# Strided extra keys in slots of their own, and one more product of 288 columns for them

## The chip, the cores and the metric

One Trainium2 chip, one of its cores. The metric is device microseconds of one execution. The kernel before takes 358.15 us, the median of 3 runs (357.57 to 358.64).

## The reference, cut to what matters

Three layers stand one behind the other. The first is attention with two masks, the second a soft mixture of experts, the third a dense layer pair with an ELU between.

```python
mask_local = (rel >= 0) & (rel < 32)                                   # heads 0 to 3
mask_strided = (rel >= 0) & (pos[None, :] % 32 == pos[:, None] % 32)   # heads 4 to 7
...                                    # softmax, attn @ v: 4 batches, 8 heads, 576 x 64
logits = x @ phi                       # 2304 x 512 by 512 x 32
slot_input = softmax(logits, 0).T @ x  # 32 slots, 4 for each of 8 experts
h = relu(slot_input[e] @ w1[e]); slot_out[e] = h @ w2[e]     # 512 -> 1024 -> 512
x = softmax(logits, 1) @ slot_out
h = x @ w_in                           # 2304 x 512 by 512 x 2048
g = where(h > 0, h, exp(min(h, 0)) - 1)
out = g @ w_out
```

In a strided head a query sees only keys of its own residue modulo 32. There are 576 / 32 = 18 keys for each residue, so a strided unit works on residues: 18 queries by 18 keys for each residue and batch.

## The kernel before, in words

All of it is one straight program. The attention is cut into 20 units, 12 local (L) and 8 strided (S), in the order `LLSLLLSSSLSSLSSLLLLL`. A unit goes through these steps: scores on TensorE (`f_qk`, L542, for a local one, two halves `f_qks`, L561, for a strided one), a softmax on VectorE and ScalarE, the division and for a strided unit the packing into `pst` on GpSimd (`f_mul`, L628), a 32x32 block transpose on VectorE (`f_tr`, L636 and L639), four copies into a block-diagonal tile `bd` on ScalarE and GpSimd (`f_sp`, L657 and L659), the products with V on TensorE (`f_pv`, L670, local; `f_pvs`, L683, strided) and the copy out of PSUM. There are two `bd` tiles for all units, three PSUM tiles `t` for the strided products and the transposes of the result, and two tiles each for scores and local products.

A strided unit holds 16 residues. Each one's 18 keys lie in 32 slots: keys 0 to 15 in the even slots, keys 16 and 17 in slots 1 and 17. V of the residue lies in the same rows of its tile, so the tile has two extra rows per batch among odd rows that are zero. These extra rows come by a load of their own (L239): 32 partitions of 2048 columns, of which three in four are zeros. One group of the product (`f_pvs(g)`) is four residues by two halves of the unit, each a product of 128 rows by 72 columns; the two halves write partitions 0 to 63 and 64 to 127 of one PSUM tile.

When the result of all units of a third of the tokens is there, TensorE makes the logits (L777) and transposes it in place (L786). Then follow the slot inputs (L413, L910), the experts' first layer (L923), their second layer (`emit_w2`, L1012) for experts 0 to 7 one behind the other, and the dense layers from L1153 on, which take the rest of the time.

The order of the work in the attention is set by a planner (`list_order`): each node has an engine, a cost, the nodes that it waits for and a key, and on each engine the ready node with the lowest key among those that can start next comes first. The keys come from a unit's due time `T[n] = T0 + TP * n + TD[n]`. The planner sets the order of the instructions alone; on the chip each engine runs its own list in that order and waits where data is missing.

All loads are issued by the sync engine, in one list. A weight load goes into a slot that an earlier tile held, and waits for the last reader of that tile: experts 1 and 2, for instance, wait for the strided scores and for the products of the first strided head pair (`q_of`, `v_of`). The dense layer's first columns (`load_head`, L348) go into the last 512 columns of four of these slots. The last weight load before the dense layers is that of expert 7's second matrix, in five parts.

Of the kernel before, what the change touches and what calls it, by code (L numbers as in the profile page):

```python
# [13 lines left out]
ALU = mybir.AluOpType  # L14
# [5 lines left out]
def attn_moe_mlp(ctx, tc, q, k, v_l, v_s, phi, w1, w2, w_in, w_out, out):  # L20
    nc = tc.nc
# [8 lines left out]
    RES = 32  # L30
    MR = S // RES
# [10 lines left out]
    T0, TP, AE = 6.0, 2.89, 0.1  # L42
    TD = (
        -32.4, -12.6, -3.1, -2.4, -7.2, 0.6, -6.0, -3.7, 1.6, -4.1,
        -0.9, -5.9, 1.6, 4.2, -2.1, 2.3, 7.2, -3.3, -9.5, 0.3,
# [31 lines left out]
    QW, WB = S * B, 4096  # L77
# [156 lines left out]
    def load_v(p, a, b):  # L234
        if p < 2:
            nc.sync.dma_start(out=VT[p][:, a:b], in_=v_l[p, :, a:b])
        else:
            nc.sync.dma_start(out=VT[p][0:128:2, a:b], in_=v_s[p - 2, 0:64, a:b])
            nc.sync.dma_start(out=VT[p][1:128:4, a:b], in_=v_s[p - 2, 64:96, a:b])  # L239
# [16 lines left out]
    with tc.manual_schedule():  # L256
# [180 lines left out]
        for n, (p, t, h) in enumerate(units):  # L437
            if p < 2:
                u = 2 * t + h
                lo_hi[n] = {"q": (384 * u, 384 * u + 384), "k": (max(384 * u - 128, 0), 384 * u + 384)}  # L440
                lo_hi[n]["v"] = lo_hi[n]["k"]
            else:
                c = 1152 * t + 576 * h
                lo_hi[n] = {"q": (c, c + 576), "k": (c, c + 576), "v": (2048 * t + 1024 * h, 2048 * t + 1024 * h + 1024)}

# [7 lines left out]
        lt = [an("G", d, [], x, f) for d, x, f in zip((0.95, 1.15, 1.15, 0.55, 1.5, 1.8), (12.0, 11.0, 11.1, 13.0, 30.0, 9.5), late)]  # L453
        RATE = 2.42
        post = []

        def load_node(kind, p, a, b, after=(), pre=None):
            f = {"q": load_q, "k": load_k, "v": load_v}[kind]
            if pre is not None:
                f = lambda *a: None  # L460
            need = min(users(p, kind, a, b))
            key = T[need] - (14 if kind != "v" else 9)
            dur = 128 * 4 * (b - a) / 1e6 * RATE
            if kind == "v" and p >= 2:
                dur *= 0.63
                after = [("n", y) for (k_, x), y in lv.items() if k_ == p and a <= x < b]
            post.append((key if pre is None else pre, dur, after, lambda: f(p, a, b), (kind, p, a, b)))
# [9 lines left out]
        for p in (2, 3):  # L477
            for x in range(2):
                h = (HW_ * x, HW_ * x + HW_)
                load_node("q", p, *h, pre=-70.0 if p == 2 and x == 0 else None)  # L480
                if p == 2 and x == 0:
                    load_node("v", p, 0, 2048)
                    continue
                load_node("k", p, *h, after=[("qk", n) for n in users(2, "k", *h)] if p == 3 else [("n", y) for y in lt[1:3]])
                load_node("v", p, 2048 * x, 2048 * x + 2048)
        for x in range(2):
            h = (HW_ * x, HW_ * x + HW_)
            load_node("q", 1, *h, after=[("qk", n) for n in users(2, "q", *h)])
            load_node("k", 1, *h, after=[("qk", n) for n in users(0, "k", *h)])
            load_node("v", 1, *h)  # L490
# [30 lines left out]
        head_node(2.5, 1, [])  # L521
# [5 lines left out]
        def unit_nodes(n):  # L527
# [91 lines left out]
            def f_mul():  # L619
# [7 lines left out]
                for a, b, o in ((0, 16, slice(0, 32, 2)), (16, MR, slice(1, 32, 16))):  # L627
                    nc.gpsimd.tensor_tensor(  # L628
                        out=z["pin"][:, :, o], in0=z["s"][:, :, a:b], in1=sm.to_broadcast([128, 16, b - a]), op=ALU.mult
                    )  # L630
# [44 lines left out]
            def f_pvs(g):  # L675
                def f():
                    pt = z["bd"]
                    og = z["o", g] = ps_t.tile([128, 512], F32, tag="t", name="so")[:, 0:4 * B * MR]
                    for j in range(4):
                        c0 = B * MR * j  # L680
                        r = 4 * g + j
                        for hh in range(2):
                            nc.tensor.matmul(  # L683
                                og[64 * hh:64 * hh + 64, c0:c0 + B * MR], v_t[p][:, t, h, hh, r, :],
                                pt[:, 8 * hh + r].rearrange("p (b m) -> p b m", b=B)[:, :, 0:MR], start=True, stop=True,
                            )
# [60 lines left out]
            vd = [x for x, y in data if y[1] == p and y[0] == "v" and n in users(p, "v", y[2], y[3])]  # L747
# [9 lines left out]
            for g in range(2):  # L757
                r = []
                y = an("P", 0.62, sp + vd, K - 7.3 + 0.6 * g, f_pvs(g), ("t", r), 32)
# [618 lines left out]
_INS = ['q', 'k', 'v_l', 'v_s', 'moe_phi', 'moe_w1', 'moe_w2', 'moe2_w_in', 'moe2_w_out']  # L1378
# [3 lines left out]
def _lay(np, q, k, v, moe_phi, **rest):  # L1382
# [10 lines left out]
    vs = v[:, 4:8].reshape(B, 2, 2, S // 32, 2, 2, 8, D).transpose(1, 0, 3, 4, 5, 2, 6, 7).reshape(2, B, S // 32, 64 * D)  # L1393
    x, z = vs[:, :, 16:], np.zeros_like(vs[:, :, 16:])
    vs = np.concatenate([x.reshape(2, -1, 64 * D) for x in (vs[:, :, 0:16], np.stack([x, z, z, z], axis=3))], axis=1)
# [4 lines left out]
    return dict(rest, q=lay(q), k=lay(k), v_l=vl, v_s=vs, moe_phi=phi, moe_w1=w1, moe_w2=w2)  # L1400
# [25 lines left out]
```

## Time and profile before

| | |
|---|---|
| median of 3 runs | 358.15 us |
| the profiled execution's own time | 357.83 us |
| its span, from the first to the last instruction | 356.1 us |
| TensorE busy | 336.8 us (95%), 2678 matmuls |
| VectorE, ScalarE, GpSimd busy | 260.8, 248.7, 57.4 us |
| moved by DMA | 70.50 MB |
| granted TensorE clock, mean | 0.998 of full speed |

Times in the rows are microseconds from the start of the span. A TensorE float32 matmul of the program shows as two matmuls in the trace (two passes), so "x32" at L683 is 16 products. A matmul's duration holds its run through the array, so several overlap; the start of the next group says how long one really holds the engine. "X idle before <-Y" is how long the engine stood still ahead of the piece, and what ended it. For a DMA, "us to landing" runs from its issue to the arrival of its last byte, with all that lies ahead of it in the queue.

### The profile page before, as it was taken

The numbers are of one execution on the slowest core, as the hardware profiler recorded it, in microseconds if no ns is written. First come the engines' busy times: TensorE is split into PE (matmuls) and PEld (weight loads), VectorE is DVE, ScalarE is ACT, GpSimd is POOL, SyncE is SP. The second block draws the span as 40 slices with busy tenths as digits, with TensorE's granted clock in tenths as the row PEclk, the third lists the DMA queues.
The fourth block names the chain that finished last, engine by engine and source line by source line (L and its number), as shares of the span: only waits on it lengthen the run. The fifth ranks groups of instructions, "written<-read, shape, count | busy, mean of one in ns | idle before, by whom it ended". The sixth has DMA issues, their size and how long they took to land.

```text
span 356.1 us, 6955 instructions
## 1 busy us (share of the span) xinstructions
PE 336.8 (95%) x2678; PEld 249.6 (70%) x2678; DVE 260.8 (73%) x574; ACT 248.7 (70%) x488; POOL 57.4 (16%) x106
## 2 busy tenths in 40 slices
PE   5589899998999999999999999999999999999995
PEld 4378777773333257787888788888878888888884
DVE  6999889743706069999999999997755674576741
ACT  9588999982216079999977877767656666666650
POOL 8888534520214000000000000000000000000000
PEclk9999999999999999999999999999999999999999
DMA  7999999999999998750006041000000030032301
GB/s 280 401 418 411 424 421 421 424 407 420 430 424 417 404 403 323 250 221 0 3 0 238 0 162 74 2 0 0 2 0 1 2 119 0 31 118 88 118 2 59
DMA packets 15328, 70.50 MB, mean 198 GB/s; under 512 B 1600, under 2 KB 2112, under 8 KB 12352
## 3 DMA queue, kind: packets, MB, share of 16 engines
q1 hardware_dynamic: 15296, 70.06, 49.3%
q8 instruction: 21, 0.34, 0.4%
q14 instruction: 11, 0.09, 0.1%
HBM read 65.34 MB, written 4.72 MB: 197 GB/s over the span
## 4 chain that ended last, share of the span: by engine, by line
PE 74%; DVE 8%; DMA 6%; ACT 4%; POOL 4%; issue 2%; DVEq 0%; SPq 0%; POOLq 0%
PE ops L1312 18%; PE ops L1314 18%; PE ops L1313 18%; DMA q<-in_moe_w_dram 6%; PE hps L1264 5%; PE s_ps L923 3%; ACT bd L657 2%; DVE sc L589 2%; PE o_ps L670 2%; PE mps L1153 1%; ACT xw L696 1%; PE xtps L786 1%; DVE sm L613 1%; POOL bd L659 1%; DVE ss L604 1%
## 5 line engine op out<-in xcount | busy, mean ns | idle before, releaser
L1274 DVE SCALAR_TENSOR_TENSOR g<-hps,g 128x512 f32<-128x512 f32 (+1 forms) x80 | 50.7, 634 | 17.8 <-ACT g L1271 17.3
L1268 ACT ACTIVATE g<-hps 128x512 f32<-128x512 f32 (+1 forms) x80 | 44.8, 560 | 13.6 <-PE hps L1264 12.2
L1271 ACT ACTIVATE g<-g 128x512 f32<-128x512 f32 (+1 forms) x80 | 47.5, 594 | 1.5
L1280 ACT ACTIVATE ghi<-g 128x512 fp32r<-128x512 f32 (+1 forms) x40 | 23.7, 591 | 18.3 <-DVE g L1274 16.5
L1314 PE MATMUL ops<-w,glo 128*128 128x512 f32 (+1 forms) x93 | 36.0, 387 | 0.0
L1280 ACT ACTIVATE rings<-g 128x512 fp32r<-128x512 f32 (+1 forms) x39 | 23.6, 606 | 17.3 <-DVE g L1274 16.5
L1312 PE MATMUL ops<-wh,rings 128*128 128x512 f32 x80 | 31.6, 396 | 0.0
L1312 PE MATMUL ops<-w,ghi 128*128 128x512 f32 (+1 forms) x81 | 31.4, 388 | 0.0
L1313 PE MATMUL ops<-w,ghi 128*128 128x512 f32 (+1 forms) x81 | 31.4, 387 | 0.0
L1313 PE MATMUL ops<-wl,rings 128*128 128x512 f32 x80 | 31.2, 390 | 0.0
L1314 PE MATMUL ops<-wh,glo 128*128 128x512 f32 x80 | 31.2, 390 | 0.0
L1264 PE MATMUL hps<-pers 128*128 128x512 f32 (+1 forms) x80 | 30.3, 380 | 0.0
L657 ACT ACTIVATE bd<-tr 32x288 f32<-32x288 f32 (+1 forms) x60 | 28.7, 479 | 1.3
L1313 PE MATMUL ops<-w,rings 128*128 128x512 f32 x64 | 25.0, 391 | 0.0
L1312 PE MATMUL ops<-w,rings 128*128 128x512 f32 x64 | 25.0, 391 | 0.0
L1314 PE MATMUL ops<-wh,rings 128*128 128x512 f32 x62 | 24.3, 392 | 0.0
L1312 PE MATMUL ops<-wh,ghi 128*128 128x512 f32 x62 | 24.2, 391 | 0.0
L1313 PE MATMUL ops<-wl,ghi 128*128 128x512 f32 x62 | 24.2, 391 | 0.0
L1314 PE MATMUL ops<-w,rings 128*128 128x512 f32 x52 | 20.2, 389 | 0.0
L1284 DVE TENSOR_TENSOR glo<-g,ghi 128x512 fp32r<-128x512 f32 (+1 forms) x24 | 15.2, 633 | 6.8 <-ACT ghi L1280 4.5
L1314 PEld LDWEIGHTS ops<-w,glo 128*128 128x128 f32 x93 | 17.5, 188 | 3.6
L670 PE MATMUL o_ps<-bd,v 128*64 128x128 f32 x288 | 18.1, 276 | 1.2 <-ACT bd L657 0.9
(230 smaller groups left out, 757.8 us busy)
## 6 DMA issues: line engine op xcount, KB each, us to landing
v<-in_moe_w_dram SPq DMA_DIRECT2D x3, 2048.0 KB, 11.8
w<-in_moe_w_in_dram SPq DMA_DIRECT2D x3, 2048.0 KB, 8.0
out_dram<-ob SPq DMA_DIRECT2D x17, 256.0 KB, 2.0
w<-in_moe_w_dram SPq DMA_DIRECT2D x2, 2048.0 KB, 11.6
xw<-in_moe_w_dram SPq DMA_DIRECT2D x4, 1024.0 KB, 11.9
xw<-in_moe_w_out_dram SPq DMA_DIRECT2D x2, 2048.0 KB, 7.8
q<-in_q_dram SPq DMA_DIRECT2D x6, 576.0 KB, 8.0
kB<-in_k_dram SPq DMA_DIRECT2D x8, 288.0 KB, 7.5
```

The source lines that it names most:

```text
L657: nc.scalar.activation(out=o, in_=i, func=AF.Copy)
L670: nc.tensor.matmul(o[64 * e:64 * e + 64, j, :], v_t[p][:, max(i - 1 + k, 0), e, :], pt[:, 4 * j + 2 * e + k], start=(k == 0), stop=(k == 1),)
L923: nc.tensor.matmul(hp[32 * g:32 * g + 32, :], siT[:, POS[c], :], w_at(2 * a + g // 2, 0, 2 * c + g % 2), start=(c == CO[0]), stop=(c == CO ...
L1264: nc.tensor.matmul(t["ps"], M4[:, 128 * f:128 * f + 128], cTf[:, t0:t0 + n], start=True, stop=True)
L1268: nc.scalar.activation(out=t["g"], in_=t["ps"], func=AF.Exp)
L1271: nc.scalar.activation(out=t["g"], in_=t["g"], func=AF.Relu, scale=-1.0, bias=1.0)
L1274: nc.vector.scalar_tensor_tensor(out=t["g"], in0=t["ps"], scalar=0.0, in1=t["g"], op0=ALU.max, op1=ALU.subtract)
L1280: nc.scalar.activation(out=t["hi"], in_=t["g"], func=AF.Copy)
L1284: nc.vector.tensor_tensor(out=t["lo"], in0=t["g"], in1=t["hi"].bitcast(F32), op=ALU.subtract)
L1312: nc.tensor.matmul(o[:, x], t["hi"][:, c], hi[:, x], start=(f == f0), stop=False)
L1313: nc.tensor.matmul(o[:, x], t["hi"][:, c], lo[:, x], start=False, stop=False)
L1314: nc.tensor.matmul(o[:, x], t["lo"][:, c], hi[:, x], start=False, stop=(f == f1 - 1 and x.stop == 512))
```

## The change

The extra keys 16 and 17 of a residue get slots that differ by residue: residue r of a group of eight takes the odd slots 2r+1 and 2r+17. So no two of eight residues share an odd slot, and the extra V rows of eight residues fit together in one compact tile of 64 columns for each half (`VX`, four tiles of 256 columns, the odd partitions; even ones are zero). A group of the strided product then begins with one more product for each half, 128 rows by 288 columns (the four residues' columns at once), and the eight products of 72 columns add to it. The odd rows of V's own tile are zero now. The 32-partition load of 2048 columns (four times) goes; a 64-partition load of 256 columns (four times) comes. Two GpSimd memsets clear the compact tiles. The fourth compact tile lies in columns 4096 to 4351 of the slot of `v2`, which was the place of the first dense columns; their load waits for the last strided product now, and its place in the list is later. The planner has a new cost for the strided product and other due times.

```diff
-    T0, TP, AE = 6.0, 2.89, 0.1
+    T0, TP, AE = -0.1, 2.858, 0.1
...
-            nc.sync.dma_start(out=VT[p][0:128:2, a:b], in_=v_s[p - 2, 0:64, a:b])
-            nc.sync.dma_start(out=VT[p][1:128:4, a:b], in_=v_s[p - 2, 64:96, a:b])
+            nc.sync.dma_start(out=VT[p][0:128:2, a:b], in_=v_s[p - 2, :, a:b])
+
+    vx = small("xt", 768, "vx", 1)
+    VX = {(2, 0): vx[:, 0:256], (2, 1): vx[:, 256:512], (3, 0): vx[:, 512:768], (3, 1): v2_sb[:, WB:WB + 256]}
+
+    def load_x(p, a, b):
+        nc.sync.dma_start(out=VX[p, a // 256][1:128:2, :], in_=v_x[p - 2, :, a:b])
...
+        lx = [an("G", 0.72, [], 9.0, lambda: nc.gpsimd.memset(vx, 0.0))]
+        lx += [an("G", 0.3, lx, 14.2, lambda: nc.gpsimd.memset(VX[3, 1], 0.0))]
...
-        head_node(2.5, 1, [])
+        head_node(5.7, 1, v_of(3))
...
-                for a, b, o in ((0, 16, slice(0, 32, 2)), (16, MR, slice(1, 32, 16))):
-                    nc.gpsimd.tensor_tensor(
-                        out=z["pin"][:, :, o], in0=z["s"][:, :, a:b], in1=sm.to_broadcast([128, 16, b - a]), op=ALU.mult
-                    )
+                nc.gpsimd.tensor_tensor(
+                    out=z["pin"][:, :, 0:32:2], in0=z["s"][:, :, 0:16], in1=sm.to_broadcast([128, 16, 16]), op=ALU.mult
+                )
+                d = z["pin"]
+                d = bass.AP(tensor=d.tensor, offset=d.offset + 1, ap=[d.ap[0], [256, 2], [34, 8], [16, MR - 16]])
+                nc.gpsimd.tensor_tensor(
+                    out=d, in0=z["s"][:, :, 16:MR].rearrange("p (e r) x -> p e r x", e=2),
+                    in1=sm.rearrange("p (e r) x -> p e r x", e=2).to_broadcast([128, 2, 8, MR - 16]), op=ALU.mult,
+                )
...
+                    cx = VX[p, t][:, 128 * h:128 * h + 128]
+                    for hh in range(2):
+                        nc.tensor.matmul(
+                            og[64 * hh:64 * hh + 64], cx[:, 64 * hh:64 * hh + 64],
+                            pt[:, 8 * hh + 4 * g:8 * hh + 4 * g + 4].rearrange("p r (b m) -> p r b m", b=B)[:, :, :, 0:MR],
+                            start=True, stop=False,
+                        )
...
-                                pt[:, 8 * hh + r].rearrange("p (b m) -> p b m", b=B)[:, :, 0:MR], start=True, stop=True,
+                                pt[:, 8 * hh + r].rearrange("p (b m) -> p b m", b=B)[:, :, 0:MR], start=False, stop=(j == 3),
...
-                y = an("P", 0.62, sp + vd, K - 7.3 + 0.6 * g, f_pvs(g), ("t", r), 32)
+                y = an("P", PVS, sp + vd, K - 7.3 + 0.6 * g, f_pvs(g), ("t", r), 40)
```

The planner's new due times change the order on all engines in the attention. Behind the product L910 TensorE's order is the same in both programs. On TensorE, from the second local value product to the first two groups of the strided one, the kernel before has these rows (`s_ps` scores, `o_ps` and `so` local and strided products with V, `lg` logits, `xtps` transposes of the result):

```order
L670 MATMUL o_ps_99<-bd,v_83 64x128 x12
L561 MATMUL s_ps_97<-kB,ex 64x72 x8
L561 MATMUL s_ps_96<-kB,ex 64x72 x8
L777 MATMUL lg<-xw,phi 32x192 x4
L786 MATMUL xtps<-ident,xw 128x128 x6
L683 MATMUL so<-bd,v_105 64x72 x8
L542 MATMUL s_ps_97<-kA,q_103 32x128 x12
L683 MATMUL so<-bd,v_105 64x72 x8
```

and the changed one these:

```order
L689 MATMUL o_ps_99<-bd,v_83 64x128 x12
L556 MATMUL s_ps_97<-kA,q_103 32x128 x12
L803 MATMUL lg<-xw,phi 32x192 x4
L812 MATMUL xtps<-ident,xw 128x128 x6
L689 MATMUL o_ps_98<-bd,v_83 64x128 x12
L575 MATMUL s_ps_96<-kB,ex 64x72 x8
L700 MATMUL so<-bd,vx 64x288 x2
L709 MATMUL so<-bd,v_105 64x72 x8
L700 MATMUL so<-bd,vx 64x288 x2
L709 MATMUL so<-bd,v_105 64x72 x8
```

The two rows L700 are new, and 16 such rows stand in the program. Ahead of the first strided product there are now three local value products (L689) and six local score blocks (L556) instead of two and five (L670, L542), and five strided score halves (L575) instead of six (L561).

On the sync engine, the weight loads of the attention's second half stand like this before (`w` expert 0, `ex` the two halves of expert 1, `v_105` expert 2 in the slot of `v2`, `kB` expert 3, `q_103` expert 4, `v_106` expert 5 in the slot of `v3`, `v_83` a part of expert 6; 512 columns of `w_in` are the dense layer's first columns):

```order
L363 DMA w_740<-in_moe_w_dram 128x4096
L363 DMA ex<-in_moe_w_dram 128x2048
L348 DMA v_105<-in_moe_w_in_dram 128x512
L348 DMA q_103<-in_moe_w_in_dram 128x512
L363 DMA v_83<-in_moe_w_dram 128x2048
L363 DMA v_105<-in_moe_w_dram 128x4096
L363 DMA ex<-in_moe_w_dram 128x2048
L363 DMA kB<-in_moe_w_dram 128x4096
L363 DMA q_103<-in_moe_w_dram 128x4096
L363 DMA v_106<-in_moe_w_dram 128x4096
```

and now like this:

```order
L369 DMA w_662<-in_moe_w_dram 128x4096
L231 DMA kB<-in_k_dram 64x1152 x2
L226 DMA q_104<-in_q_dram 128x1152
L369 DMA ex<-in_moe_w_dram 128x2048
L354 DMA q_103<-in_moe_w_in_dram 128x512
L369 DMA v_83<-in_moe_w_dram 128x2048
L369 DMA ex<-in_moe_w_dram 128x2048
L369 DMA kB<-in_moe_w_dram 128x4096
L369 DMA v_105<-in_moe_w_dram 128x4096
L369 DMA q_103<-in_moe_w_dram 128x4096
L369 DMA v_106<-in_moe_w_dram 128x4096
L354 DMA kB<-in_moe_w_in_dram 128x512
```

Expert 2's load of 2 MB (`v_105`) has moved behind the second half of expert 1 (`ex`) and expert 3 (`kB`), which both wait for the last strided scores.

## Rows read from the trace of the kernel before

**Rows 1.** Chain that ended last: start, length, engine, tile, line.

```profile
89.77 7.07 PE s_ps L923 x64
...
101.08 0.29 SPq L363
101.41 22.16 DMA q<-in_moe_w_dram
123.62 2.34 PE o_ps L1012 x8
```

**Rows 2.** Windows: stretch, length, busy time by engine (instructions), clock, DMA share, GB/s.

```profile
5.00:25.00 20.00, 12.50 (x273) 10.66 (x273) 17.88 (x58) 14.66 (x28) 17.20 (x22) 1.00 1.02 406
25.00:65.00 40.00, 36.44 (x788) 30.01 (x786) 36.21 (x113) 37.48 (x83) 22.11 (x42) 1.00 1.02 420
65.00:80.00 15.00, 14.94 (x211) 11.40 (x208) 8.25 (x34) 13.75 (x33) 7.32 (x11) 1.00 0.99 411
...
126.00:356.00 230.00, 226.22 (x1054) 181.63 (x1053) 179.20 (x320) 166.82 (x319) 0.00 (x0) 1.00 0.22 83
```

**Rows 3.** Timeline of TensorE, experts' second layer: start, length, line, shapes.

```profile
113.30 1.90 PE L1012 MATMUL o_ps<-ex,h1T_b 128*32 128x512 f32 x16
115.01 1.90 PE L1012 MATMUL o_ps<-v,h1T_b 128*32 128x512 f32 x16
...
118.04 1.07 PE L1012 MATMUL o_ps<-kB,h1T_b 128*32 128x512 f32 x8
...
120.74 1.05 PE L313 MATMUL wps<-ident 128*128 128x256 bf16 x8
121.72 1.66 PE L1012 MATMUL o_ps<-q,ss 128*32 128x512 f32 x8
...
125.89 0.83 PE L313 MATMUL wps<-ident 128*128 128x256 bf16 x6
```

**Rows 4.** Page, section 6: DMA issues, count, KB each, median us to landing.

```profile
out_dram<-ob SPq DMA_DIRECT2D x17, 256.0 KB, 2.0
...
v<-in_v_s_dram SPq DMA_DIRECT2D x4, 256.0 KB, 7.8
...
phi<-in_moe_phi_dram SPq DMA_DIRECT2D x1, 64.0 KB, 5.6
```

**Rows 5.** Timeline of TensorE in the attention.

```profile
18.92 0.67 PE L561 MATMUL s_ps<-kB,ex 128*64 128x72 f32 x16
19.52 0.86 PE L542 MATMUL s_ps<-kA,q 128*32 128x128 f32 x24
20.31 1.53 PE L670 MATMUL o_ps<-bd,v 128*64 128x128 f32 x24
21.68 0.67 PE L561 MATMUL s_ps<-kB,ex 128*64 128x72 f32 x16
...
25.77 0.72 PE L683 MATMUL so<-bd,v 128*64 128x72 f32 x16
...
63.75 1.22 PE L683 MATMUL so<-bd,v 128*64 128x72 f32 x32
64.80 1.48 PE L670 MATMUL o_ps<-bd,v 128*64 128x128 f32 x24
```

**Rows 6.** Timeline of GpSimd, a memset of 768 columns.

```profile
0.80 0.74 POOL L260 MEMSET kA<- 128x768 f32 x1 [0.29 <-POOLq L1410]
```

**Rows 7.** Page, section 5: ScalarE's copies into the block-diagonal tile.

```profile
L657 ACT ACTIVATE bd<-tr 32x288 f32<-32x288 f32 (+1 forms) x60 | 28.7, 479 | 1.3
```

**Rows 8.** Timeline of the sync engine: issues of weight loads.

```profile
51.02 0.33 SPq L363 DMA_DIRECT2D ex<-in_moe_w_dram  x1
...
93.44 0.33 SPq L363 DMA_DIRECT2D w<-in_moe_w_dram  x1
```

**Rows 9.** DMA issues of the windows 50:60 and 93.4:93.6, those two loads' landing.

```profile
ex<-in_moe_w_dram SPq DMA_DIRECT2D x1, 1024.0 KB, 9.1
...
w<-in_moe_w_dram SPq DMA_DIRECT2D x1, 2048.0 KB, 11.4
```

More of the change, by code (lines that the diff above doesn't have):

```diff
@@ L19, in attn_moe_mlp @@
 @with_exitstack
-def attn_moe_mlp(ctx, tc, q, k, v_l, v_s, phi, w1, w2, w_in, w_out, out):
+def attn_moe_mlp(ctx, tc, q, k, v_l, v_s, v_x, phi, w1, w2, w_in, w_out, out):
     nc = tc.nc
@@ L30, in attn_moe_mlp @@
     RES = 32
+    PVS = 1.1
     MR = S // RES
@@ L41, in attn_moe_mlp @@
     FIFO = ("sp", "sl", "ss", "cb", "pst", "mx", "sm", "tr", "bd", "o", "qw", "t", "l")
-    T0, TP, AE = 6.0, 2.89, 0.1
+    T0, TP, AE = -0.1, 2.858, 0.1
     TD = (
-        -32.4, -12.6, -3.1, -2.4, -7.2, 0.6, -6.0, -3.7, 1.6, -4.1,
-        -0.9, -5.9, 1.6, 4.2, -2.1, 2.3, 7.2, -3.3, -9.5, 0.3,
+        -35.5, -18.2, -0.3, -9.8, -1.4, 0.8, -3.0, -3.4, 4.9, -9.2,
+        -6.5, 5.9, -3.5, 4.1, -1.0, 4.2, 4.4, -1.2, -4.4, 8.0,
     )
@@ L441, in attn_moe_mlp @@
                 lo_hi[n]["v"] = lo_hi[n]["k"]
+                lo_hi[n]["x"] = (0, 0)
             else:
@@ L444, in attn_moe_mlp @@
                 lo_hi[n] = {"q": (c, c + 576), "k": (c, c + 576), "v": (2048 * t + 1024 * h, 2048 * t + 1024 * h + 1024)}
+                lo_hi[n]["x"] = (256 * t + 128 * h, 256 * t + 128 * h + 128)
         def users(p, kind, a, b):
@@ L457, in load_node @@
         def load_node(kind, p, a, b, after=(), pre=None):
-            f = {"q": load_q, "k": load_k, "v": load_v}[kind]
+            f = {"q": load_q, "k": load_k, "v": load_v, "x": load_x}[kind]
             if pre is not None:
@@ L461, in load_node @@
             need = min(users(p, kind, a, b))
-            key = T[need] - (14 if kind != "v" else 9)
+            key = T[need] - {"v": 9.0, "x": 8.9}.get(kind, 14.0)
             dur = 128 * 4 * (b - a) / 1e6 * RATE
+            if kind == "x":
+                dur *= 0.53
             if kind == "v" and p >= 2:
-                dur *= 0.63
+                dur *= 0.5
                 after = [("n", y) for (k_, x), y in lv.items() if k_ == p and a <= x < b]
@@ L482, in attn_moe_mlp @@
                     load_node("v", p, 0, 2048)
+                    load_node("x", p, 0, 256, after=[("n", lx[0])])
                     continue
@@ L485, in attn_moe_mlp @@
                 load_node("v", p, 2048 * x, 2048 * x + 2048)
+                load_node("x", p, 256 * x, 256 * x + 256, after=[("n", lx[p == 3 and x == 1])])
         for x in range(2):
@@ L746, in unit_nodes @@
             rel["tr"] += sp
-            vd = [x for x, y in data if y[1] == p and y[0] == "v" and n in users(p, "v", y[2], y[3])]
+            vd = [x for x, y in data if y[1] == p and y[0] in "vx" and n in users(p, y[0], y[2], y[3])]
             if local:
@@ L1375, in attn_moe_mlp @@
             nodes[n][4]()
-_INS = ['q', 'k', 'v_l', 'v_s', 'moe_phi', 'moe_w1', 'moe_w2', 'moe2_w_in', 'moe2_w_out']
+_INS = ['q', 'k', 'v_l', 'v_s', 'v_x', 'moe_phi', 'moe_w1', 'moe_w2', 'moe2_w_in', 'moe2_w_out']
 _OUTS = [((2304, 512), 'float32')]
@@ L1391, in _lay @@
     vl = v[:, 0:4].reshape(B, 2, 2, S // 32, 32, D).transpose(1, 0, 4, 3, 2, 5).reshape(2, 128, 4 * S)
-    vs = v[:, 4:8].reshape(B, 2, 2, S // 32, 2, 2, 8, D).transpose(1, 0, 3, 4, 5, 2, 6, 7).reshape(2, B, S // 32, 64 * D)
-    x, z = vs[:, :, 16:], np.zeros_like(vs[:, :, 16:])
-    vs = np.concatenate([x.reshape(2, -1, 64 * D) for x in (vs[:, :, 0:16], np.stack([x, z, z, z], axis=3))], axis=1)
+    vs = v[:, 4:8].reshape(B, 2, 2, S // 32, 2, 2, 8, D).transpose(1, 0, 3, 4, 5, 2, 6, 7)
+    vx = vs[:, :, 16:].transpose(0, 1, 2, 6, 3, 4, 5, 7).reshape(2, 64, 8 * D)
+    vs = vs[:, :, 0:16].reshape(2, 64, 64 * D)
     phi = moe_phi.reshape(4, 128, -1).transpose(1, 0, 2).reshape(128, -1)
@@ L1399, in _lay @@
               for w in (rest["moe_w1"], rest["moe_w2"]))
-    return dict(rest, q=lay(q), k=lay(k), v_l=vl, v_s=vs, moe_phi=phi, moe_w1=w1, moe_w2=w2)
+    return dict(rest, q=lay(q), k=lay(k), v_l=vl, v_s=vs, v_x=vx, moe_phi=phi, moe_w1=w1, moe_w2=w2)
 def kernel(**inputs):
```

## The prediction, before the changed kernel ran

> **What bounds the kernel now.** I read the chain of waits first, from its end backwards. From 123.62 on it is TensorE almost without a break [rows 1], busy 226.22 of the 230 us behind 126 [rows 2]; the change touches nothing there, so what counts is when that part begins. Just ahead of it the chain leaves TensorE: the sync engine issues expert 7's second matrix at 101.08, as soon as its slot is free, and the data take 22.16 us [rows 1]. That is a queue, not a slow transfer: the windows show all DMA engines full from 5 on (share 0.99 to 1.02, 406 to 420 GB/s) [rows 2]. So the start of the dense part is set by bytes ahead of that matrix over rate.
>
> TensorE runs close behind. In the second layer an undisturbed expert takes 115.01 - 113.30 = 1.71 us. Expert 6 takes 120.74 - 118.04 = 2.70, and expert 7, from 121.72 to the next work at 125.89, 4.17 [rows 3]. The excess, 0.99 + 2.46 = 3.45 us, is all that TensorE waits for weights, since the fillers (L313) between are in the program anyway. So two paths lead to 125.89: the loads, with no slack, and TensorE from the attention on, with 3.45 us. The third view is the attention in windows: TensorE is busy 12.50 of 20 us in 5 to 25, 36.44 of 40 in 25 to 65 and 14.94 of 15 in 65 to 80. In the first stretch VectorE is nearly full (17.88 of 20), in the second ScalarE (37.48 of 40) [rows 2].
>
> **The change part by part.** *Loads.* Four loads of 256 KB [rows 4] become four of 64 KB (64 partitions, 256 columns, 4 bytes: an estimate from the shapes), 0.79 MB less, at 420 GB/s 1.87 us. Count and issue time on the sync engine stay, since one issue replaces one. A small load isn't free in itself, but in a full queue it costs its bytes: that of phi, 64 KB, landed in 5.6 us, no later than a 256 KB load (7.8) [rows 4]. The Trainium skill speaks against this part: DMA: Bandwidth & Descriptors, section Bandwidth, has 64 KB transfers at 0.95 us and calls smaller ones descriptor-dominated. By that figure, an estimate, four would take 3.8 us and the loads would lose 1.3 instead of gaining 1.9; the row of phi doesn't show it.
>
> *The new products.* 16 groups get one product of 288 columns for each of two halves. Bounds: the first layer's 512-column products take 7.07 us for 64 passes, four at a time, 0.44 a round [rows 1]; 288 columns in two passes are then 0.50 us with the halves side by side. The eight old products of a group hold the engine (64.80 - 63.75) / 2 = 0.525 for the same columns per half [rows 5]; if the halves ran one behind the other it would be about 1.0. I take 0.50, as the nearest row also streams wide: 16 x 0.50 = 8.0 us more on TensorE, all between 25 and 70. The upper end is 16.
>
> *What hides of that.* First, the new order. Ahead of the first strided product TensorE has now done one local score block more (20.31 - 19.52 = 0.79), one local value block more (21.68 - 20.31 = 1.37) and one strided score half less (19.52 - 18.92 = 0.60) [rows 5]: 1.56 us of work drawn into a stretch with idle time. This holds if that product comes no later than 25.77 [rows 5]; VectorE has 12 instructions more ahead of its transpose, at most 12 x 17.88 / 58 = 3.7 us [rows 2], but before, the product came some time behind it. GpSimd (17.20 of 20 busy) gets two memsets, 0.74 for 768 columns [rows 6] and a third of that for 256: 1.0 us. I put 0.4 us on the first product for both, between 0 and 3. Second, idle time behind 25: 40 - 36.44 + 15 - 14.94 = 3.6 us [rows 2]. It goes only where ScalarE has the next tile ready. The product holds its `bd` tile twice as long, and the copies into the next one (4 x 0.479 us [rows 7]) can't begin sooner. I let 1.0 of the 3.6 stay, between 0 and 3.6. So the attention ends 8.0 - 1.56 + 0.4 - 2.6 = 4.2 us later (bounds 2.8 and 9.4, by these edits alone).
>
> *Moved loads.* Expert 2's 2 MB now stand behind two loads that wait for the last strided scores. On the sync engine all later weights queue behind such a wait. The load issued at 51.02 [rows 8] landed 9.1 later, 1 MB [rows 9]: less 2.5 for its own bytes at 420 GB/s and about 1.4 of latency (256 KB on an empty queue land in 2.0 us [rows 4], 0.6 of it bytes), 5.2 us lay ahead of it. Expert 2 (5.0), a head of dense columns (0.6) and the saving (1.87) are missing there now, 7.5 us: if the scores come at the same time, the queue stands empty for 2.3 us, which eats the saving. They stand earlier in TensorE's list by work, so I take a hole of 0 to 2.3, 0.8 likely. The load at 93.44 landed 11.4 later, 2 MB, so 11.4 - 5.0 - 1.4 = 5.0 us lay ahead [rows 8, 9]; with TensorE 4.2 later and the queue 1.87 less a hole of 0.8 earlier the slack is gone and 0.3 us of hole come. So the loads end 1.87 - 0.8 - 0.3 = 0.8 us earlier. The dense columns' own load, moved behind, is read only after the first layer (from 89.77 [rows 1]) and bytes ahead of expert 7 stay the same: nothing. The division's other pattern on GpSimd writes as many elements: nothing, at most 0.2 a unit, under the same cover of ScalarE.
>
> *Sum.* The dense part begins when the later path ends: loads -0.8, TensorE 4.2 - 3.45 = +0.75. TensorE becomes the bound. On the profiled execution that is 357.83 + 0.75 = 358.6 (span 356.1 and 1.7 around it, as now); the median shown lies 0.3 above the profiled time, so I predict **358.9 us**. About 0.3%, 1.07 us, is what a measurement of this kernel can tell from no change.
>
> **Rivals.** *Slower: the second tile isn't ready.* Place: `bd` copies on ScalarE between 25 and 65. For it: two tiles for all units, ScalarE busy 94% there [rows 2]; against: ScalarE gets 4 us more time for the same work. If none of the idle time is used the attention ends 8.0 - 1.56 + 0.4 = 6.8 us later, the dense part 3.4: 361.5. It decides from 3.45 + 1.07 = 4.5 us late.
>
> *Faster: the products are hidden.* If more early work is drawn forward (7.5 us stand idle in 5 to 25 [rows 2]) and the rest of the idle time is used, TensorE ends less than 1.6 us late and the bytes decide: 358.15 - 1.87 = 356.3. For it: the order was moved as a whole; against: VectorE is full in that stretch and its work is the same, and TensorE alone has no idle time behind 65.
>
> *No gain by the queue.* TensorE is in time, but the hole at 51 takes the saving: 358.15 + 2.3 - 1.87 = 358.6. For it: the 7.5 against 5.2 us above; against: the scores need be only 2.3 us earlier.
>
> *Small loads hold the queue.* If the four new loads cost what the old ones did, nothing is saved: the loads end 1.87 later than in the sum, 1.1 behind now, and the time is 359.2 by rows, at the edge of the bound. Against: phi's row [rows 4]. By the page named above they would lose 1.3 us more, which gives 360.5.
>
> *The halves don't overlap.* The wide products cost 16 us instead of 8, and the time is 8 us above the forecast, 367. Against: the 72-column pairs do overlap on the same halves, as their 0.525 us a group shows [rows 5].
>
> **How the numbers follow.** Forecast 0.43 (358.0 to 359.9; 0.31 of it within the bound, 0.12 slower), tile not ready 0.23 (slower), hidden 0.20 (faster), the queue 0.10 (same), small loads 0.02 (slower), no overlap 0.02 (slower). That gives faster 0.20, same 0.41, slower 0.39. The range for 8 in 10 reaches from the hidden case to just short of the full slow one, 356.4 to 361.3; the forecast's own is 358.0 to 359.9.
>
> **What would show it.** The new products: 32 products (64 matmuls) at about 0.25 us a pass, 0.50 a group. The attention: the first matmul of the experts' first layer, now at 89.77, at about 94. The second layer: experts 6 and 7 at 1.71 us each, without waits for DMA. The loads: expert 7's matrix there before TensorE asks. Wrong would be an attention that ends less than 2 or more than 6 us later, DMA waits still at experts 6 and 7 (then the loads bound it), or a DMA share well under 1 between 48 and 56 (then the queue's hole).

## The result, and the profile after

The changed kernel takes 363.31 us (median of 4 runs, 362.50 to 363.63), the one before 358.15 beside it (median of 3; a fourth execution, of 383.28, is a slow one and left out): ratio 1.0142, 95% interval 1.0113 to 1.0170, slower by 4.1 to 6.1 us. Predicted were 358.9 us, 356.4 to 361.3. The profiled execution took 363.12 us, 5.29 more than that of before, and the dense part begins 5.27 later. Behind that start nothing changed: the profiled time less the start is 231.9 to 232.1 us in the kernels below, so each can be read by when its dense part begins.

The windows of after, columns as in [rows 2]:

```profile
5.00:25.00 20.00, 15.59 (x278) 12.94 (x280) 17.26 (x57) 14.10 (x26) 17.12 (x23) 1.00 1.01 393
25.00:65.00 40.00, 35.84 (x752) 29.28 (x751) 35.09 (x112) 34.36 (x76) 21.33 (x42) 1.00 0.96 390
65.00:80.00 15.00, 14.65 (x220) 10.78 (x222) 5.49 (x17) 13.76 (x29) 8.30 (x13) 1.00 0.93 371
...
126.00:356.00 230.00, 229.77 (x1078) 181.77 (x1071) 177.72 (x317) 166.84 (x319) 0.00 (x0) 1.00 0.24 90
```

Two things stand against [rows 2]. TensorE has 8 us more to do and still idles more behind 25: 4.16 + 0.35 = 4.5 us, where it was 3.6. And the DMA engines, full before, are not: shares 0.96 and 0.93.

The experts' second layer on TensorE, answering to [rows 3]:

```profile
124.63 1.92 PE L1038 MATMUL o_ps<-kB,h1T_b 128*32 128x512 f32 x16
126.49 1.05 PE L319 MATMUL wps<-ident 128*128 128x256 bf16 x8
127.47 1.17 PE L1038 MATMUL o_ps<-q,ss 128*32 128x512 f32 x8
128.86 2.36 PE L1038 MATMUL o_ps<-q,ss 128*32 128x512 f32 x8 [0.23 <-DMA q<-in_moe_w_dram]
131.16 0.83 PE L319 MATMUL wps<-ident 128*128 128x256 bf16 x6
```

Expert 6 no longer waits, so TensorE itself is late here: 124.63 against 118.04. But expert 7 (127.47 to 131.16) still takes 3.69 us instead of some 1.8, so the loads are late as well and end last, in spite of 0.79 MB less (69.71 MB moved, 70.50 before).

The new products (L700), in a stretch without waits, and the sync engine's issues that answer to [rows 8]:

```profile
53.66 0.66 PE L700 MATMUL so<-bd,vx 128*64 128x288 f32 x4
54.14 0.67 PE L709 MATMUL so<-bd,v 128*64 128x72 f32 x16
54.64 0.66 PE L700 MATMUL so<-bd,vx 128*64 128x288 f32 x4
55.13 0.67 PE L709 MATMUL so<-bd,v 128*64 128x72 f32 x16
```

```profile
50.26 0.33 SPq L369 DMA_DIRECT2D ex<-in_moe_w_dram  x1
50.69 0.37 SPq L369 DMA_DIRECT2D kB<-in_moe_w_dram  x1
55.84 0.33 SPq L369 DMA_DIRECT2D v<-in_moe_w_dram  x1
56.22 0.43 SPq L369 DMA_DIRECT2D q<-in_moe_w_dram  x1
69.02 0.33 SPq L369 DMA_DIRECT2D v<-in_moe_w_dram  x1
...
100.03 0.33 SPq L369 DMA_DIRECT2D w<-in_moe_w_dram  x1
```

A wide pair costs 54.14 - 53.66 = 0.48 us, the next one 0.49. The load at 69.02 is that of expert 5's first layer, into the slot of the second strided V tile; it waits for the last strided products. In the kernel before it was issued at 65.04:

```profile
65.04 0.33 SPq L363 DMA_DIRECT2D v<-in_moe_w_dram  x1
```

Where the queue is empty in after (length, then the last two columns, share and GB/s), and below it the same stretches before:

```profile
48.00:56.00 8.00, 6.67 (x159) 5.65 (x158) 7.02 (x21) 6.27 (x14) 2.50 (x6) 1.00 0.73 276
65.00:70.00 5.00, 4.65 (x81) 3.33 (x81) 3.06 (x11) 4.88 (x10) 3.24 (x5) 1.00 0.85 344
68.00:76.00 8.00, 8.00 (x118) 6.03 (x116) 2.56 (x8) 6.98 (x16) 4.49 (x7) 1.00 0.84 323
100.00:106.00 6.00, 6.00 (x57) 1.88 (x52) 3.14 (x8) 1.88 (x3) 0.00 (x0) 1.00 0.91 329
```

```profile
48.00:56.00 8.00, 7.75 (x169) 5.99 (x171) 7.49 (x25) 7.75 (x17) 3.74 (x6) 1.00 1.03 428
65.00:70.00 5.00, 4.94 (x72) 3.76 (x70) 3.47 (x14) 4.87 (x12) 4.37 (x6) 1.00 0.98 419
68.00:76.00 8.00, 8.00 (x119) 6.49 (x117) 3.24 (x15) 7.66 (x17) 4.89 (x8) 1.00 0.99 413
100.00:106.00 6.00, 6.00 (x56) 2.03 (x52) 0.43 (x4) 1.19 (x2) 0.63 (x1) 1.00 1.01 429
```

By the share the queue is empty for 2.2 us in 48 to 56, 1.3 in 68 to 76 and 0.5 in 100 to 106, each around one of those issues. The rate falls further than the share: against the kernel before 2.5 MB are missing in these three stretches, at 420 GB/s some 6.0 us.

### The profile page after: what moved, and what is told of

Read it like the earlier page. It is cut to its first block, busy times and chain, and to the rows that moved or that the text cites. A ratio compares the mean times of both kernels' runs of the same rounds, so it can differ in the third digit from the quotient of the medians.

```text
span 361.4 us, 7086 instructions
## 1 busy us (share of the span) xinstructions
PE 344.9 (95%) x2742; PEld 255.7 (71%) x2742; DVE 260.3 (72%) x574; ACT 249.9 (69%) x488; POOL 57.5 (16%) x108
## 2 busy tenths in 40 slices
DMA packets 15456, 69.71 MB, mean 193 GB/s; under 512 B 1600, under 2 KB 2368, under 8 KB 12608
## 4 chain that ended last, share of the span: by engine, by line
PE 75%; ACT 8%; DMA 7%; DVE 7%; issue 1%; SPq 1%; DVEq 0%; ACTq 0%
PE ops L1338 18%; PE ops L1340 18%; PE ops L1339 18%; DMA q<-in_moe_w_dram 6%; PE hps L1290 5%; ACT bd L676 4%; PE s_ps L949 3%; PE o_ps L689 2%; PE xtps L812 2%; ACT xw L722 2%; DVE sc L603 2%; DMA kA<-in_k_dram 1%; PE mps L1179 1%; PE lg L803 1%; PE wps L1399 1%
## 5 line engine op out<-in xcount | busy, mean ns | idle before, releaser
L1310 DVE TENSOR_TENSOR glo<-g,rings 128x512 fp32r<-128x512 f32 (+1 forms) x24 | 15.1, 630 | 5.5 <-ACT rings L1306 4.8
```

The source lines that it names most:

```text
L1310: nc.vector.tensor_tensor(out=t["lo"], in0=t["g"], in1=t["hi"].bitcast(F32), op=ALU.subtract)
```

## The experiments

Three numbers of the profiled execution go with each time below: when the first product of the slot inputs starts (L910 before, 88.92; L936 after, 95.51), when TensorE alone would be through with expert 7, and when the dense part begins. The second is the start of expert 6 plus 4.69 us, which is what experts 6 and 7 with their fillers take where no load is late:

| kernel | us, median | ratio to before, 95% | slot inputs | TensorE alone | dense part |
|---|---|---|---|---|---|
| before | 358.15 | | 88.92 | 122.73 | 125.89 |
| before_one_load_less | 355.11 | 0.9904 to 0.9933 | 88.01 | 121.82 | 121.82 |
| before_early_load_less | 357.40 | 0.9965 to 0.9993 | 88.74 | 122.55 | 125.71 |
| product_old_order | 360.28 | 1.0051 to 1.0088 | 92.24 | 126.05 | 127.66 |
| change_old_order | 361.74 | 1.0076 to 1.0125 | 93.07 | 126.88 | 129.74 |
| old_order_gate_moved | 359.97 | 1.0037 to 1.0085 | 92.44 | 126.25 | 127.36 |
| after | 363.31 | 1.0113 to 1.0170 | 95.51 | 129.32 | 131.16 |
| after_one_load_less | 361.49 | 1.0079 to 1.0106 | 96.16 | 129.97 | 129.97 |
| after_gate_moved | 362.29 | 1.0096 to 1.0137 | 95.85 | 129.66 | 131.55 |
| thin_products | 364.41 | 1.0156 to 1.0195 | 96.29 | 130.10 | 133.41 |
| change_old_cost | 364.67 | 1.0165 to 1.0246 | 97.89 | 131.70 | 131.83 |
| change_old_due_times | 369.04 | 1.0275 to 1.0331 | 99.46 | 133.27 | 136.22 |

### First question: the products, or the order?

**no_product**: the changed kernel without its 32 wide products (the extra keys' part is left out).

```diff
-                    for hh in range(2):
-                        nc.tensor.matmul(og[64 * hh:64 * hh + 64], cx[:, 64 * hh:64 * hh + 64], ..., start=True, stop=False)
```

> The changed kernel without its 32 products of 288 columns (keys 16 and 17 of each residue are left out of the strided heads' result); order, loads and memsets as changed. Theory (A): the 8 us of products are what makes the attention end 6.6 us later, as TensorE's waits there are for VectorE and ScalarE and can't be filled; then the releases come late and the DMA queue runs dry. Without them the first layer starts at 89 to 90.5 (changed: 96.4), DMA waits at experts 6 and 7 are those of before less the bytes, and the time is 356.5 to 358.5. Rival (B): the new order costs by itself (the third local score block waits for its keys, TensorE stands still and is slow till 17.8): then the first layer starts at 91 or later and the time stays above 359. Rival (C): the moved loads cost by themselves: the attention ends in time, but the hole in the queue at 48 to 52 stays and expert 7 comes as late as before or later, 358.5 to 360.

(The eight 72-column products of a group start their own sums again.) Measured: 363.55 us, ratio 1.0138 to 1.0213, as slow as with the products; the slot inputs come at 96.93. The theory that 8 us of products make the lateness falls at once. What TensorE no longer does it waits for, with 28.93 of 40 us busy:

```profile
25.00:65.00 40.00, 28.93 (x684) 24.82 (x684) 33.95 (x107) 32.34 (x72) 20.92 (x40) 1.00 0.92 369
```

**product_old_order**: the kernel before and its order, with 32 such products on a cleared tile.

```diff
+                    for hh in range(2):
+                        nc.tensor.matmul(og[64 * hh:64 * hh + 64], zx[:, 64 * hh:64 * hh + 64], ..., start=True, stop=False)
```

> The kernel before with the 32 products alone, on a zeroed tile (they add nothing to the result); order, loads and due times of before. (A): the attention ends 5 to 7 us later, first layer at 95 to 97, time 362 to 364, even without the new order. (B): the products mostly fit into the old order's gaps, first layer before 93.2 (3.45 later than before), time below 359.5.

Measured: 360.28 us, between the two theories, and the slot inputs 3.3 us later. Of 8.0 us of products the old order hides 4.7. The prediction's terms for what is hidden add up to 1.56 + 2.6 - 0.4 = 3.8: near, for an order that it did not speak of.

**new_due_times**: the kernel before with the three tables of due times of after.

```diff
-    T0, TP, AE = 6.0, 2.89, 0.1
+    T0, TP, AE = -0.1, 2.858, 0.1
```

(and `TD` likewise)

> The kernel before with the changed kernel's due times alone (T0, TP, TD); no product, loads of before but in the order that the due times give. (A): within 1 us of before, 357.4 to 359.4. (B): 359.5 or more, with TensorE at the lower level past 15 us and the first layer at 91 or later. (C): 358.5 to 360 with a hole in the queue near 50.

Measured: 359.26 us, ratio 1.0021 to 1.0049: the time of theory (A), but the slot inputs 2.8 us later (91.71) without a single new product, which is (B). An order alone can make TensorE nearly as late as the products do.

**thin_products** settles what no_product left: there, taking instructions away may change more than their time. The products stay, on 18 columns (the extra keys' part is left out).

```diff
-                            og[64 * hh:64 * hh + 64], cx[:, 64 * hh:64 * hh + 64], pt[...288 columns...], start=True, stop=False,
+                            og[64 * hh:64 * hh + 64, 0:MR], cx[:, 64 * hh:64 * hh + 64], pt[:, 8 * hh + 4 * g, 0:MR], start=True, stop=True,
```

> The changed kernel in its own order, each wide product cut from 288 columns to 18 (the extra keys' part is left out); the count of products and all tiles stay. Theory order: still above 360 us, the experts' first layer no earlier than 93 us (it was 95.5 after, 88.9 before). Rival products: some 7.5 us of TensorE go, so the first layer starts near 88.5 and the time is 357 to 358.5.

Measured: 364.41 us. It is not a clean subtraction: VectorE's two strided transposes near 40 us, which follow one another in after at 38.06 and 40.00, stand apart here,

```profile
37.40 0.71 DVE L658 STREAM_TRANSPOSE tr<-pst 128x512 f32<-128x512 f32 x1
42.12 0.71 DVE L658 STREAM_TRANSPOSE tr<-pst 128x512 f32<-128x512 f32 x1 [2.68 <-ACT bd L676]
```

by a wait of 2.68 us for ScalarE that after does not have (no_product has it too; why the wait differs was not tried). Taking all 2.68 off the slot inputs still leaves 93.6, later than before by 4.7. So with this order TensorE's load does not set the attention's pace; the waits between the engines do. How much each single wait costs was not tried.

**change_old_order**: the whole change, every engine in the order of before (the compact loads take the place of the old ones in the list, and VectorE clears the compact tiles at the start instead of GpSimd).

```diff
-    T0, TP, AE = -0.1, 2.858, 0.1
+    T0, TP, AE = 6.0, 2.89, 0.1
...
-                y = an("P", PVS, sp + vd, K - 7.3 + 0.6 * g, f_pvs(g), ("t", r), 40)
+                y = an("P", 0.62, sp + vd, K - 7.3 + 0.6 * g, f_pvs(g), ("t", r), 32)
```

> The whole change (64 compact V rows in slots of their own, 32 wide products, first dense columns loaded behind the last strided products) but with every engine's instructions in the order of the kernel before. Theory order (the new order on the engines, not the products, costs most of the 5 us): as the products alone in the old order, 360.3 us, between 359.6 and 360.7, since 0.79 MB less brought nothing in compact_rows. Rival products (8 us of TensorE that nothing hides): 363 us. Rival loads (the saved bytes do count, 1.87 us): 358.4 us.

Measured: 361.74 us (360.38 to 363.57), above its range and 1.5 above product_old_order. TensorE's waits of 25 to 80, in this kernel and then in after (waiting for whom: us, times, longest):

```profile
PE so L691 <- ACT bd L667: 0.7, 1, 0.7
PE so L691 <- ACT xw L815: 0.6, 1, 0.6
```

```profile
PE s_ps L556 <- DVE sc L603: 2.3, 2, 1.3
PE so L700 <- ACT bd L676: 1.3, 3, 0.6
PE o_ps L689 <- ACT bd L676: 0.5, 1, 0.5
PE so L700 <- ACT xw L824: 0.4, 1, 0.4
```

The old order leaves 1.3 us of waits, the new one 4.5; the slot inputs differ by 2.4. The larger half of the new waits is for VectorE: a local score block can't start since VectorE hasn't emptied the score tile (L603, its copies of strided scores).

**change_old_due_times** and **change_old_cost** are two more orders of the same change: the old tables of due times with the new cost, and the new tables with the old cost.

```diff
-    PVS = 1.1
+    PVS = 0.62
```

(change_old_cost, with 32 for 40 instructions; the other has the old `T0`, `TP` and `TD`)

> The changed kernel with the due times (T0, TP, TD) of before and all else of its own, so the planner makes a third order. Theory order (what the change costs beyond products and late gates comes from how this order lets TensorE wait for VectorE and ScalarE): between change_old_order and after or outside them by what TensorE idles in 25 to 65 us: 1.5 us idle gives 361.7, 4.2 us idle gives 363.3. Rival: the due times don't matter, 363.3 whatever it idles.

> The changed kernel with its own due times, the planner told the old cost of a strided group (0.62 and 32 instructions), so a fourth order. Theory order: the time follows TensorE's idle share in 25 to 65 us by the same rule (1.5 idle: 361.7; 4.2 idle: 363.3). Rival: the costs told to the planner don't matter, 363.3.

Measured: 369.04 and 364.67 us, with 7.3 and 6.6 us of TensorE idle between 25 and 80. Over four orders of the same work the idle time and the time rise together (1.5, 4.5, 6.6, 7.3 against 361.7, 363.3, 364.7, 369.0), but not at one rate; my rule would have given 364.1 and 363.6. The worst one has a second cause, its queue. A load of expert 1 waits there until 64.64, and the window of 25 to 65 says what that is worth:

```profile
25.00:65.00 40.00, 34.49 (x689) 27.58 (x691) 29.11 (x85) 30.33 (x66) 18.86 (x38) 1.00 0.76 305
```

### Second question: why are the loads late?

**compact_rows**: the kernel before, with its extra V rows loaded as 8 partitions of 2048 columns instead of 32, the zeros left out: the change's 0.79 MB less, without its products and its order.

```diff
-            nc.sync.dma_start(out=VT[p][1:128:4, a:b], in_=v_s[p - 2, 64:96, a:b])
+            nc.sync.dma_start(out=VT[p][1:128:16, a:b], in_=v_s[p - 2, 64:72, a:b])
```

> The kernel before, its extra V rows loaded as 8 partitions of 2048 columns (the rows that are not zero) instead of 32: the same 0.79 MB saved as in the change, no product, no new order. If bytes ahead of expert 7 set the start of the dense part, and TensorE has 3.45 us of slack: expert 7 lands 1.9 us earlier, time 356.3 to 356.8. If the bytes of these loads are hidden anyway (or holes eat them): 358.0 to 358.7. If 8 partitions keep only a few DMA engines busy and that costs more than the bytes save: above 358.7.

Measured: 358.15 us, ratio 0.9985 to 1.0025: nothing, with the queue never empty by its share:

```profile
5.00:25.00 20.00, 13.31 (x264) 11.99 (x264) 17.10 (x56) 14.19 (x27) 16.76 (x22) 0.91 1.02 386
25.00:65.00 40.00, 36.37 (x783) 29.54 (x780) 36.11 (x114) 37.49 (x82) 22.60 (x42) 1.00 1.02 406
```

The shares are those of [rows 2], the rates 386 and 406 GB/s instead of 406 and 420: the saved bytes came back as a lower rate. A share near 1 doesn't say that the rate is all that can be had. Whether the 8 partitions themselves lowered the rate stays open here; what bytes in this place are worth is asked again below, without them (before_early_load_less).

**after_one_load_less** and **before_one_load_less**: without the 2.1 MB of expert 4's second layer (the buffer's old content is used). That is 5.0 us of queue at 420 GB/s, late in the list: the load is issued at 93.86 before and at 100.46 in after, behind the stretches of 48 to 76.

```diff
+            if (e, second) == (4, 1):
+                return
```

> The changed kernel without the 2.1 MB load of expert 4's second layer (it computes with what the buffer held): 5.0 us less in the queue behind it. If the start of the dense part waits for expert 7's halves by what the trace names (about 2.0 us in all) and TensorE's own path ends near 129.2 us: 361.3 us, 2.0 less than after. If the waits only mirror something else on TensorE: 363.3. If more than 2.5 us go, TensorE's path had more slack than read.

> The same load left out of the kernel before. The prediction's two paths: the loads path moves 5 us earlier and TensorE's, with 3.45 us of slack, then decides: 354.7 us, 3.4 less. If the dense part's own loads decide anyway: 358.

Measured: 361.49 and 355.11 us, 1.8 less than after and 2.9 less than before. Of after_one_load_less:

```profile
125.28 1.92 PE L1040 MATMUL o_ps<-kB,h1T_b 128*32 128x512 f32 x16
127.13 1.05 PE L319 MATMUL wps<-ident 128*128 128x256 bf16 x8
128.11 1.92 PE L1040 MATMUL o_ps<-q,ss 128*32 128x512 f32 x16
129.97 0.83 PE L319 MATMUL wps<-ident 128*128 128x256 bf16 x6
```

No wait is left and the four pieces take 4.69 us; so TensorE alone is through at 124.63 + 4.69 = 129.32 in after, 3.4 of the 5.3 us, and the loads add 1.84. In the kernel before, TensorE's slack is 125.89 - 122.73 = 3.16 us, and with the load left out TensorE decides, so the 2.9 us are not all that the loads gained.

**before_early_load_less**: as many bytes left out early, expert 2's first layer (issued at 45.80; the piece at 42.83, which the expectation names, is one of expert 6's).

```diff
+            if (e, second) == (2, 0):
+                return
```

> The kernel before without a 2.1 MB load that is issued early, at 42.83 us: expert 2's first layer (it computes with what the buffer held). Theory gates (the queue stops at 51.02 for a buffer that TensorE frees, so bytes issued ahead of that only lengthen the stop): no gain, 357.7 to 358.3 us. Rival bytes (the loads path is a sum of bytes, as the prediction took it): 3 us less, as before_one_load_less, which left out as many bytes behind the last stop: 355.1 us.

Measured: 357.40 us, 0.3 to 1.25 us less, where the late load won 2.4 to 3.4. The queue just runs empty later on:

```profile
25.00:65.00 40.00, 36.34 (x788) 29.90 (x789) 36.11 (x114) 37.50 (x83) 21.99 (x43) 1.00 0.99 400
65.00:80.00 15.00, 14.95 (x209) 11.35 (x207) 8.24 (x32) 13.75 (x33) 7.25 (x11) 1.00 0.94 356
```

So the queue has stops, loads that wait for a buffer that TensorE frees, and bytes ahead of a stop are almost free. The change's saving is all ahead of them: its last small load is issued at 25.29.

**before_head_later**: the kernel before, with the first dense columns loaded where after loads them.

```diff
-        head_node(2.5, 1, [])
+        head_node(5.7, 1, v_of(3))
```

> The kernel before with one thing of the change: 0.26 MB of the first dense columns are issued behind the last strided products (near 65.5 us) instead of at 36.65 us. Theory gates: these 0.6 us of queue move from ahead of a stop to behind it, 358.6 us, 0.6 more than before. Rival bytes: nothing is added, 358.0 us.

Measured: 358.21 us, ratio 0.9984 to 1.0013. No 0.6 us: this part of the change costs nothing that can be measured here, and my rule for it was too simple.

**delay_ahead_of_gate** and **delay_behind_gate** ask which stop it is. 24 idle TensorE passes in the kernel before, ahead of the experts' first layer (which frees the buffer of the load at 93.44) or ahead of expert 6's second; the edit of the first:

```diff
-        warm(W9, wps_)
+        warm(W9 + 12, wps_)
```

> The kernel before with 24 idle TensorE passes (128x256, about 0.115 us each by the fillers in its trace, 2.8 us in all) put between the layer-one input and the experts' first layer, nothing else changed. Theory gate: the load of expert 3's second layer (issued at 93.44 us) waits for TensorE's first layer, so the loads move with TensorE: the dense part starts 2.3 to 2.8 us later, 360.4 to 360.9 us. Rival, the prediction's picture of two separate paths: TensorE has 3.2 us of slack at the end, so 358.1 us.

> The kernel before with 24 idle TensorE passes more (some 2.4 to 2.8 us) ahead of expert 6's second layer, that is behind the last load that TensorE releases. Both pictures say here that TensorE's slack of 3.2 us hides them: 358.1 us, 358.6 at most. If they cost 2.5 us, the slack was misread and the dense part waits for TensorE, not for expert 7's halves.

Measured: 358.41 and 357.93 us, ratios 0.9979 to 1.0015 and 0.9980 to 1.0013. My theory of that gate falls. The load was issued at 95.56 instead of 93.44, and the queue had work all the time:

```profile
94.00:96.00 2.00, 2.00 (x24) 0.65 (x20) 1.27 (x2) 0.32 (x1) 0.00 (x0) 1.00 1.02 418
96.00:100.00 4.00, 4.00 (x40) 1.30 (x36) 1.05 (x3) 1.45 (x3) 0.00 (x0) 1.00 1.04 408
```

**delay_ahead_of_last_products**: 30 such passes ahead of products of the last strided head pair, and so ahead of expert 5's load. In the trace they stand at 59.23 and take 3.43 us, ahead of the products that came at 57.60 before; TensorE's last strided products, those of 63.75, follow at 68.47.

```diff
+                    if n == of[3][-1] and g == 0:
...
+                        for _ in range(30):
+                            nc.tensor.matmul(og[:, 0:256], wm[:, 0:128], wm, start=True, stop=True)
```

> The kernel before with 30 idle TensorE passes (3.45 us) ahead of the last strided unit's products (63.75 us), nothing else changed. The gate is now taken to be the load of expert 5's first layer, which waits for these products (65.04 us): it is issued 3.4 us later, the queue runs dry, the loads path is 1.4 to 2.0 us late as in product_old_order (gate 3.45 us late, start of the dense part 1.77 late): 359.5 to 360.2 us. Rival, separate paths: TensorE's own path, 3.45 later with 3.16 of slack, gives 0.3: 358.4 us.

Measured: 360.68 us (358.71 to 361.75), above its range; ratio 1.0037 to 1.0079, 1.3 to 2.8 us, where separate paths would give 0.3 for these passes. The profiled execution is a long one, 361.75: its first strided product is 1.6 us late already, and TensorE alone would be through at 127.45, 4.7 later than before, for which separate paths would give 1.6. The dense part begins at 129.81, 3.9 later; the last 2.4 are the loads'. Expert 5's load is issued at 69.76, and the windows show the empty queue (0.98 and 0.97 before):

```profile
65.00:70.00 5.00, 4.96 (x123) 3.99 (x122) 4.69 (x18) 4.86 (x12) 1.19 (x2) 1.00 0.91 382
70.00:75.00 5.00, 4.94 (x72) 3.63 (x66) 3.41 (x13) 4.87 (x12) 4.21 (x6) 1.00 0.85 321
```

**old_order_gate_moved**, **before_gate_moved**, **after_gate_moved**: in change_old_order, before and after, three loads whose buffers are free sooner (2.4 MB) are issued ahead of expert 5's instead of behind it.

```diff
-            w_node(7, 7, 9, a, b, k1_of(a, b))
+            w_node(4.5, 7, 9, a, b, k1_of(a, b))
...
-        head_node(5.5, 7, q_of(3))
+        head_node(4.4, 7, q_of(3))
```

> change_old_order with three loads (expert 7's first layer in two halves and 0.26 MB of dense columns, 2.4 MB, whose buffers are free by 66.7 us) issued ahead of expert 5's, which waits until 69.3 us. Theory gate: the queue has work over the stop, the loads win back 1.2 to 1.8 us: 360 to 360.5 us; no less than 358.9, where TensorE's own path ends. Rival (the lateness comes from elsewhere): 361.7 us.

> The same move of loads in the kernel before, whose queue shows no stop at 65 to 80 us (share 0.99). Theory gate: nothing to win, 358.1 us, within 0.3. Rival: if the place of these loads matters by itself, it shows here, over 0.5 either way.

> The same move of loads in the changed kernel. Theory gate: the stop at 68 to 72 us (about 1.0 us of empty queue) goes; 362.3 us, no less than 361.4, where TensorE's own path ends. Rival: 363.3 us.

Measured: 359.97 us (1.8 less than without the move), 358.18 (nothing) and 362.29 (1.0 less), all three medians within 0.1 us of what the gate says. The window of 65 to 70 in change_old_order, and then with the loads moved:

```profile
65.00:70.00 5.00, 5.00 (x104) 3.86 (x95) 4.93 (x19) 4.25 (x11) 1.57 (x3) 1.00 0.67 280
```

```profile
65.00:70.00 5.00, 5.00 (x98) 3.91 (x99) 4.78 (x18) 4.26 (x11) 1.51 (x4) 1.00 0.98 399
```

In the old order the profiled executions agree: the dense part begins at 127.36 instead of 129.74, and only 0.6 of that is TensorE's. The times themselves spread (two of the six with the moved loads took 361.7), and the intervals of the two ratios overlap by a little. In after the profiles don't agree: the stop at 65 to 70 is gone there too (share 0.97, was 0.85), but expert 7 comes as late against TensorE as it did (131.55 - 129.66 = 1.9), and the intervals of the two ratios overlap there too. So the gate behind the last strided products is shown in the old order, by the profiles more than by the times; in the new one, with the stop at 48 to 56 still there (share 0.66, was 0.73), it is one of several, and its price there is open.

No version of the change beats the kernel before; the best is old_order_gate_moved, 1.3 to 3.0 us slower.

## Why the prediction was wrong, point by point

**What bounds the kernel.** Right: the dense part's start decides, loads and TensorE lead to it, and TensorE has slack (3.16 us by before_one_load_less; predicted 3.45). Wrong was to take the two as separate.

**The products.** Right: about 0.50 us a group, halves side by side, 8.0 us.

**What hides of them.** The first failed step: "the attention ends 8.0 - 1.56 + 0.4 - 2.6 = 4.2 us later". The experts' first layer was to begin near 94 and begins at 96.37, 6.6 us later. The term that failed is the idle time behind 25: of 3.6 us I let 1.0 stay, and 4.5 are there. product_old_order shows that the old order does take up the idle time (1.5 left); it is the new order that makes new waits. The first strided product came at 27.00, 1.2 later where I took 0.4. With both terms as measured the sum would be 8.0 - 1.56 + 1.2 + 0.9 = 8.5, some 1.9 too much: the wait of 0.41 ahead of 27.00 stands in both terms, the 72-column products hold TensorE for 8.9 us instead of 9.6 (by the starts of the rows behind them), and 0.8 stay open. Ahead of that first product TensorE is also slower for longer than before: 24 passes of local scores take 1.51 us at 11.84 and 0.86 at 19.82, while before 48 passes take 1.52 at 12.85, though the granted clock reads 1.00 in 5 to 25 in both. What this adds to the 1.2 us was not tried. Reading the old profile's idle time as room is right only for the old order.

**The loads.** The second failed step, and the one that sets the time: "the loads end 1.87 - 0.8 - 0.3 = 0.8 us earlier". They end 5.27 us later. The saved 1.87 us stand ahead of the stops, where bytes are almost free (before_early_load_less; compact_rows agrees). The hole that I put near 51 with 0.8 us, between 0 and 2.3, is 2.2 by the share, close to its upper end: expert 2's load now stands behind the wait for the strided scores, and the queue runs dry from 48 on. In change_old_order, which keeps that load ahead of the wait, the share of 48 to 56 is 1.02. The hole at 100 is 0.5 where I took 0.3. The hole that I had no term for is the one behind the last strided products, 1.3 us: I moved their end by 4.2 us in the one path and left the load that waits for them, 65.04, where it was in the other. With these three the sum is 1.87 - 2.2 - 1.3 - 0.5, 2.1 us later. The other 3.1 us lie in rates: within the three stretches the rate fell further than the share (6.0 us by the rate, 4.0 by the share), and the rest came in lower rates at a full share, as 393 GB/s against 406 in 5 to 25 and 397 against 420 in 80 to 90. Why the rate is lower is open, and no run moved expert 2's load alone back ahead.

All three signs of being wrong that I had named are there: the attention ends over 6 us later, expert 7 waits for a DMA at 128.86, and the share of 48 to 56 is 0.73.

**The rivals.** The slower one, "the second tile isn't ready", priced TensorE's path at +3.4 us, and TensorE alone is 129.32 - 125.89 = 3.4 late. Its mechanism was half of it: of 4.5 us of waits 1.8 are for the `bd` copies, 2.3 for VectorE's copies of the scores, and the loads then add 1.84 us that it did not have. "No gain by the queue" was right that the saving goes, and its hole of 2.3 us is close to the 2.2 measured, but it had TensorE in time. "Small loads" is not needed for it: in after the four loads of 64 KB land 6.8 us (three) and 7.8 us after their issue, the V loads of 512 KB beside them in 7.3. "Hidden" and "no overlap" are out.

**The moved dense columns.** Right: nothing (before_head_later).

## What to carry to other kernels

Bytes have a price by where they stand in the queue: 2.1 MB left out late in the queue won 2.9 us, as many ahead of the stops 0.75. So when a change delays an engine, follow each load that waits for what it frees, and ask how much work the queue still holds when that wait begins; 2.1 us of delay at one such load cost nothing, 3.4 us of passes ahead of another cost 1.3 to 2.8. Follow as well what a load moved behind such a wait leaves missing ahead of it. And idle time in a profile belongs to its order of instructions: a change that comes with a new order has to be priced with the new waits, or tried in the old order first; here four orders of the same work lie 7.3 us apart.

## What the runs showed that I had not expected

A load that moves fewer bytes over fewer partitions need not shorten the queue: with 8 partitions instead of 32 in four loads the two stretches ran at 386 and 406 GB/s instead of 406 and 420, and the time stayed. And taking work off one engine can add a wait on another: with the products thinned, a VectorE transpose waited 2.68 us for ScalarE where it had not waited.
